# Chunk 0 of a scan stacked on 128 partitions, weight bits in PSUM, and last outputs on two queues, in a fused scan and two-MLP kernel

## The chip, the cores and the metric

One core of a Trainium2 chip. The metric is the device time of one launch in microseconds; the kernel before takes 570.02 us (median of three runs, 569.48 to 570.22).

## The reference

An attention-like scan over 4 batches, 8 heads, 768 positions, head size 32 and state size 16, then two MLPs over the 3072 tokens, width 256, hidden width 2048:

```python
L  = np.exp(cum[:, :, :, None] - cum[:, :, None, :]) * causal   # cum: running sum of log a
M  = np.einsum('bhin,bhjn->bhij', Cc, Bc) * L
y  = M @ xc + (Cc @ state) * np.exp(cum)                        # chunk by chunk
state = decay_full * state + sum_j(Bc_j x_j * decay_from_j)
h  = x @ w_in;  x = (h / (1 + np.exp(-1.702 * h))) @ w_out      # first MLP, x = y of all heads
h  = x @ w_in;  out = (h * np.clip(h + 3, 0, 6) / 6) @ w_out    # second MLP
```

Inputs of the scan are float32; the weights of the MLPs arrive as float64.

## The kernel before

**The scan.** The 768 positions are cut into 8 chunks of 96, so that there are 32 pieces q = 4c + b (chunk c, batch b), each with all 8 heads. A piece works on E = 112 rows: 96 positions of the chunk and the 16 rows of the state. Per piece and group g of four heads: `decay` (DVE, L450) makes the 112 x 448 matrix of decays by a scan over the row of `a`, with a constant pattern `pat_sb` that restarts it; for the first six pieces the row is spread over the partitions by four matmuls (`a_spread`, L440) into PSUM, for later ones by a DMA into SBUF. `s_mm` (PE, L485) makes the scores of two pieces. They are multiplied with the decays by DVE (`g_mul`, L488) or copied by ACT (`g_copy`, L491) and multiplied by POOL (`g_pool`, L495). `y_mm` (PE, L511) makes y and the new state; ACT copies the state (`y_state`, L525) and the high part of y (`y_out`, L545) and DVE makes the low part (`y_lo`, L557); `st_turn` (DVE, L561) transposes the state for the next chunk. In chunk 0 all of a piece's 112 rows are worked, over all 112 columns, though rows 96 to 111 hold no state yet (`zero_xs`) and the part below the diagonal of a causal matrix is zero.

**The MLPs.** The 3072 tokens are cut into blocks of 512. Everything is kept in two parts (high and low, both read by PE as fp32r), so that a product is three matmuls. The first blocks go in *units*, one of 16 weight slices with one block: `l1` (L672, 6 matmuls: low x with high weight, high x with high weight, high x with low weight), an activation chain (`act_chain`, ACT L675, L684 and DVE or POOL L687), and `l2` (L697, 6 matmuls); later blocks go in a Strassen-like form (L833). A weight slice p is loaded by SP (`w_load`, L353, 512 KB) and decoded: `w_scale` (ACT, L357), `w_low` (ACT L362 or DVE L364: the three bits that the float32 needs of the second word), `w_join` (DVE, L368: shifts and joins both words, two SBUF operands), `w_top` (L371, ACT, DVE or POOL), `w_bottom` (POOL, L375).

```python
low = raw(p)[:, :, 0]                                                        # L361
nc.vector.scalar_tensor_tensor(B_(f"dec:{p}"), t[:, :, 1], 3, t[:, :, 0], ALU.logical_shift_left, ALU.bitwise_or)   # L368
```

**The order.** `Schedule.run` is a list scheduler that runs when the program is built: each step is added with engine, estimated length, due time (`PIECE`, `tu`, `DL`, `TH`, `TL`) and what it reads and writes, and the steps of each engine stand in the order it finds. Buffers come from small pools; PSUM has two banks `h`, four `acc`, one `s` and one `y`. `decode(p, ...)` adds the steps of a slice.

**The start and the end.** Before the first piece, ACT issues the loads of the constants and of four row tables (L398, L400, L465) and loads its function table (L389); 12 warm-up matmuls run on PE. At the end, `outs` (L860 to L872) scales the two halves of each block's result (`o_scale`: ACT L853, DVE L855) and stores them (`o_store`, L858), on SP, the last half's first 256 columns on ACT.

## Time and profile before

| | |
|---|---|
| median of three runs | 570.02 us |
| the profiled execution | 570.0 us, span 568.2 us |
| mean granted TensorE clock | 0.985 |
| busy: PE, DVE, ACT, POOL | 553.7 (97%), 427.8 (75%), 331.3 (58%), 299.2 (53%) us |
| busy DMA, whole span | 37.7 MB, 66 GB/s on average |

The span is what the profiler saw of the program; 1.8 us of the launch lie outside it. A busy PE is one with matmuls in flight. A clock of 1.00 is 2.4 GHz, 0.50 is 1.2 GHz.

### The profile page before, as it was taken

How to read it: one execution, taken by the hardware profiler on the slowest of the kernel's cores; microseconds unless marked ns; L12 is line 12 of the kernel's file. 1: busy time of each engine (PE TensorE's matmuls, PEld its weight loads, DVE VectorE, ACT ScalarE, POOL GpSimd, SP SyncE). 2: the span in 40 equal slices, each digit the busy share in tenths (PEclk: the TensorE clock that was granted, in tenths of full speed). 3: DMA queues.
4: the chain of work that ended last, by engine and by line, in shares of the span. 5: the costliest groups of instructions: out<-in, count | busy, mean ns of one | idle time of the engine just before them, and what ended most of it. 6: DMA issues, size and time to landing. Idle time of an engine off the chain costs nothing.

```text
span 568.2 us, 8940 instructions
## 1 busy us (share of the span) xinstructions
PE 553.7 (97%) x3292; PEld 449.5 (79%) x3292; DVE 427.8 (75%) x617; ACT 331.3 (58%) x608; POOL 299.2 (53%) x281
## 2 busy tenths in 40 slices
...
GB/s 172 386 175 192 84 99 85 42 114 74 91 84 161 62 2 0 181 100 18 37 2 114 109 37 1 0 2 1 75 1 1 0 1 0 76 1 1 0 1 74
DMA packets 21995, 37.71 MB, mean 66 GB/s; under 512 B 10544, under 2 KB 14112, under 8 KB 21952
## 3 DMA queue, kind: packets, MB, share of 16 engines
...
q10 hardware_dynamic: 1136, 0.48, 0.4%
q8 instruction: 26, 0.43, 0.3%
q14 instruction: 17, 0.14, 0.1%
...
## 4 chain that ended last, share of the span: by engine, by line
PE 93%; DVE 3%; DMA 2%; ACT 1%; issue 1%; SPq 0%; DVEq 0%; ACTq 0%
PE acc L697 46%; PE h L833 19%; PE h L672 15%; PE s L833 4%; PE y L833 4%; PE s L485 2%; PE h L511 1%; DVE dec L368 1%; DMA bx_w<-in_wu 1%; DMA ov_a<-in_bcz 1%; DVE ov_a L450 1%; PE s L511 0%; PE y L511 0%; PE acc L485 0%; PE acc L672 0%
## 5 line engine op out<-in xcount | busy, mean ns | idle before, releaser
L687 POOL TENSOR_TENSOR gl<-gg,gh 128x512 fp32r<-128x512 f32 x42 | 60.8, 1447 | 96.2 <-ACT gh L684 40.5
L697 PE MATMUL acc<-gh,wl 128*128 128x512 f32 x256 | 100.1, 391 | 0.0
L697 PE MATMUL acc<-gh,wh 128*128 128x512 f32 x256 | 99.8, 390 | 0.0
L845 DVE TENSOR_TENSOR ov_b<-h,ov_b 128x512 f32<-128x512 f32 x64 | 44.1, 689 | 53.8 <-PE h L833 53.2
L697 PE MATMUL acc<-gl,wh 128*128 128x512 f32 x256 | 80.2, 390 | 0.5 <-DVE gl L687 0.5
L697 PE MATMUL acc<-ov_b,wh 128*128 128x512 f32 x256 | 78.8, 389 | 0.0
L450 DVE TENSOR_TENSOR_SCAN ov_a<-ov_a,pat_sb 112x448 f32<-112x448 f32 x52 | 65.6, 1298 | 0.0
L687 DVE TENSOR_TENSOR gl<-h,gh 128x512 fp32r<-128x512 f32 x60 | 41.0, 685 | 24.7 <-ACT gh L684 23.6
L687 POOL TENSOR_TENSOR ov_b<-ov_b 128x512 fp32r<-128x512 f32 x24 | 31.6, 1316 | 49.6 <-ACT ov_b L684 49.5
L697 PEld LDWEIGHTS acc<-gl,wh 128*128 128x128 f32 x256 | 48.0, 188 | 10.9 <-DVE gl L687 0.9
L697 PEld LDWEIGHTS acc<-gh,wl 128*128 128x128 f32 x256 | 48.0, 188 | 10.5 <-issue 0.2
L697 PEld LDWEIGHTS acc<-ov_b,wh 128*128 128x128 f32 x256 | 48.1, 188 | 10.0
L697 PEld LDWEIGHTS acc<-gh,wh 128*128 128x128 f32 x256 | 48.1, 188 | 9.9
L375 POOL TENSOR_TENSOR wl<-dec,wh 128x512 fp32r<-128x512 f32 x32 | 44.5, 1393 | 19.0 <-ACT wh L371 14.4
L678 ACT ACTIVATE gg<-h 128x512 f32<-128x512 f32 x48 | 28.7, 598 | 42.6 <-PE h L833 36.0
L675 ACT ACTIVATE h<-h 128x512 f32<-128x512 f32 x44 | 25.6, 583 | 45.2 <-PE h L672 35.8
L697 PE MATMUL acc<-ov_b,wl 128*128 128x512 f32 x128 | 49.8, 389 | 0.0
L684 ACT CAST gh<-gg 128x512 fp32r<-128x512 f32 x66 | 40.9, 620 | 11.8 <-DVE gg L681 10.6
L684 ACT CAST gh<-h 128x512 fp32r<-128x512 f32 x60 | 35.2, 588 | 16.2 <-DVE h L681 13.9
L687 POOL TENSOR_TENSOR ov_b<-gg,ov_b 128x512 fp32r<-128x512 f32 x16 | 21.1, 1319 | 43.1 <-ACT ov_b L684 30.7
L675 ACT ACTIVATE gg<-h 128x512 f32<-128x512 f32 x34 | 20.3, 598 | 38.9 <-PE h L672 38.5
L368 DVE SCALAR_TENSOR_TENSOR dec<-bx_w 128x512 uint32<-128x512 uint32 x32 | 34.3, 1079 | 3.2 <-ACT bx_w L357 1.8
(262 smaller groups left out, 1314.3 us busy)
## 6 DMA issues: line engine op xcount, KB each, us to landing
...
```

The lines of the kernel that those rows point to most:

```text
L368: nc.vector.scalar_tensor_tensor(B_(f"dec:{p}"), t[:, :, 1], 3, t[:, :, 0], ALU.logical_shift_left, ALU.bitwise_or)
L375: e.tensor_tensor(out=lo, in0=B_(f"dec:{p}").bitcast(F32), in1=hi.bitcast(F32), op=ALU.subtract)
L450: nc.vector.tensor_tensor_scan(t, a, pat_sb, 0.0, ALU.mult, ALU.add)
L485: nc.tensor.matmul(out=s_bank(q, g)[:, k, :], lhsT=t[r:r + NS, 0, i], rhs=t[r:r + NS, 1, i], start=True, stop=True)
L672: nc.tensor.matmul(out=B_(hn(u)), lhsT=w[:, 128 * j:128 * j + 128], rhs=x[:, j], start=x is xl and j == 0, stop=low and j == 1)
L675: nc.scalar.activation(B_(dst), B_(src), AF.Gelu_apprx_sigmoid)
L678: nc.scalar.activation(B_(dst), B_(src), AF.Relu, bias=3.0)
L684: nc.scalar.copy(B_(dst), B_(src))
L687: e.tensor_tensor(out=B_(dst), in0=B_(src), in1=B_(hi).bitcast(F32), op=ALU.subtract)
L697: nc.tensor.matmul(out=B_(acc[d]), lhsT=w[:, 256 + 128 * d:384 + 128 * d], rhs=g, start=first and d not in seen, stop=last and d not in [v ...
L833: nc.tensor.matmul(out=B_(dst), lhsT=w, rhs=x, start=start and i == 0, stop=i == 2, skip_group_check=True)
L845: nc.vector.tensor_tensor(out=B_(dst), in0=B_(a), in1=B_(b), op=ALU.add)
```

## The change

1. **Chunk 0 in stacked rows.** For its four pieces, rows 0 to 63 of two batches are stacked on 128 partitions (`x_spread` PE L488, `x_decay` DVE L517 with the pattern `patx`, `sx_mm` PE L535, `gx_mul` DVE L548 or `gx_copy` ACT L551 and `gx_pool` POOL L554). Rows 64 to 95 of all four batches are stacked on 128 partitions and only columns 64 to 111 are worked (`y_spread` L495, `y_decay` L520 with `paty`, `sy_mm` L544, `gy_mul` L557). `yx_mm` (PE, L569) makes y of two batches with 64 small matmuls into the banks h, h, s and y. New constants: `patx` by an ACT DMA (L422), `paty_sb` by another (L424) and `paty_spread` on POOL (L416), three selectors cast by ACT (`sel_rows`, L480), `ay_part` (ACT, L472). `pat_sb` moves behind these. ACT now loads a function table twice. The load of x is three DMAs (`x0_load`), `zero_xs` goes.
2. **Low bits in PSUM.** For slices 0 to 8 `w_low` writes the bits to bank s or y (`w_bits`), and `w_join` reads one operand from there. The scheduler's mark for steps that exclude POOL is off for these joins.
3. **Order.** `l1` of unit 0 is split: high x first, then low x, then the low weight. Pieces 6 to 9 are visited one by one (`SOLO`) and not in pairs. Several due times and choices of engine change (`PK`, `WAFTER`, `DL`, `TH`, `TL`, `GMS`, `TOPV`); `l2` of the last blocks is split by output half.
4. **Last outputs.** The second-last block's ACT half is stored by ACT's queue; the last block's halves change engines and are each cut in columns 128 to 511 (SP) and 0 to 127 (SP and ACT).

The core of the diff (the decays, scores and products of chunk 0, part 1, are shown by their adds and two functions):

```diff
 
 
-DL = (4.5, 1.3, 0.6, 1.6, 0.6)
-TOPV = (2, 5, 8, 11)
-TOPP = (2, 3, 7, 24, 27, 28, 31)
+LP = 9
...
-UGAP = (12, 0.25)
+P0 = (4.8, 9.0)
...
     i = (q >= 12) + (q >= 16) + (q >= 22)
     return PK[2 * i] + PK[2 * i + 1] * (q - (6, 12, 16, 22)[i])
 
-WAFTER = (2.9, 4.9, 6.9, 11.0, 13.0, 15.0, 17.0)
+WAFTER = (2.4, 4.5, 5.1, 9.7, 10.0, 17.7, 22.7)
 TURN = 30.0
 HACC = (2, 3)
...
+    def w_bits(p):
+        return B_(f"{'sy'[p % 2]}:low{p}").bitcast(U32) if p < LP else raw(p)[:, :, 0]
+
     def w_low(p, act):
-        low = raw(p)[:, :, 0]
+        low = w_bits(p)
         if act:
             nc.scalar.activation(low, raw(p).bitcast(U8)[:, :, 3], AF.Copy, scale=1 / 32, bias=-31 / 64)
         else:
-            nc.vector.tensor_scalar(low, low, 29, None, ALU.logical_shift_right)
+            nc.vector.tensor_scalar(low, raw(p)[:, :, 0], 29, None, ALU.logical_shift_right)
 
     def w_join(p):
         t = raw(p)
-        nc.vector.scalar_tensor_tensor(B_(f"dec:{p}"), t[:, :, 1], 3, t[:, :, 0], ALU.logical_shift_left, ALU.bitwise_or)
+        nc.vector.scalar_tensor_tensor(B_(f"dec:{p}"), t[:, :, 1], 3, w_bits(p), ALU.logical_shift_left, ALU.bitwise_or)
 
     def w_top(p, e):
...
+            nc.scalar.dma_start(out=patx(), in_=pat[0:64, 0:4 * E].bitcast(BF16).unsqueeze(0).to_broadcast([2, 64, 4 * E]))
+        elif i == 3:
+            nc.scalar.dma_start(out=paty_sb, in_=pat[0:32, 0:E - 64].bitcast(BF16).unsqueeze(0).to_broadcast([4, 32, E - 64]))
         else:
             nc.scalar.dma_start(out=idn_sb, in_=idn)
 
     add("POOL", 0.3, -90, zero_state, w=["st_sb"])
     add("POOL", 0.35, -75, selectors, r=["idn"], w=["sel"])
     add("-", 0.0, -95, lambda: None, w=["att"])
...
+    def sel_rows(i):
+
+        nb, q0 = ((2, 0), (2, 2), (NB, 0))[i]
+        src = idn_sb[0:NB * 4, NS + NH + 4 * q0:NS + NH + 4 * q0 + 4 * nb].rearrange("r (b q) -> r q b", q=4).unsqueeze(3).to_broadcast([NB * 4, 4, nb, 128 // nb])
+        nc.scalar.copy(B_(SX[i])[0:NB * 4].rearrange("r (q b n) -> r q b n", q=4, b=nb), src)
+
+    def sel_of(i, qh):
+        return B_(SX[i])[0:NB * 4, 128 * qh:128 * qh + 128]
+
+    def x_spread(p, g):
+        for i in range(2):
+            for part in range(2):
+                nc.tensor.matmul(out=B_(f"acc:lx{p}.{g}")[:, 2 * E * i:2 * E * i + 256], lhsT=sel_of(p, 2 * g + i),
+                                 rhs=B_("gh:acl")[0:NB * 4, 256 * part:256 * part + 256], start=part == 0, stop=part == 1)
...
+    def yx_mm(p):
+
+        x = B_("xs:0")
+        for g in range(2):
+            for late in range(2):
+                for k in range(4):
+                    h = 4 * g + k
+                    for b in (2 * p, 2 * p + 1):
+                        r, n, c, i = (32 * b, 32, 64, 2) if late else (64 * (b % 2), 64, 0, p)
+                        gm = gmy()[r:r + n, h, :] if late else gmx(p, g)[r:r + n, k, :]
+                        nc.tensor.matmul(out=y_view(b)[32 * k:32 * k + 32, g, c:E], lhsT=x[r:r + n, i, h * D:(h + 1) * D], rhs=gm,
+                                         start=not late, stop=bool(late), skip_group_check=True)
 
     def a_spread(q, g):
...
+        if q < NB and b % 2 == 0:
+            p = q // 2
+            t = KX[p]
+            sch.take(f"l:x{p}", t)
+            for g in range(2):
+                add("PE", 0.48, t - 1 + 0.1 * g, x_spread, p, g, r=["gh:acl", "al", SX[p]], new=[f"acc:lx{p}.{g}"])
+                add("DVE", 1.06, t + 0.1 * g, x_decay, p, g, r=[f"acc:lx{p}.{g}", f"l:x{p}", "gg:patx"], w=[f"lx{p}.{g}"])
+            add("PE", 1.0, t + 0.9, sx_mm, p, r=["r16:0"] + rows[0], new=[SBANK(q, g) for g in range(2)])
+            for g in range(2):
+                sn, gn = SBANK(q, g), f"gm:x{p}.{g}"
+                if 2 * p + g in GMX:
+                    add("ACT", 0.55, t + 1.2 + 0.1 * g, gx_copy, p, g, r=[sn], new=[gn])
+                    add("POOL", 1.16, t + 1.2 + 0.1 * g, gx_pool, p, g, r=[f"l:x{p}", f"lx{p}.{g}"], w=[gn])
+                else:
...
         R, Dn, W = f"bx:w{p}", f"dec:{p}", f"wt:{p}"
         k -= DL[4] if p < NM else 0.0
+        low = dict(new=[f"{'sy'[p % 2]}:low{p}"]) if p < LP else dict(w=[f"low{p}"])
         add("SP", 0.4, k - 9, w_load, p, new=[R], kb=512, after=after)
         add("ACT", 0.72, k - DL[0], w_scale, p, r=[R], w=[f"hi{p}"])
         if LOW(p) == "ACT":
-            add("ACT", 0.70, k - DL[1], w_low, p, True, r=[R], w=[f"low{p}"])
-        else:
-            add("DVE", 0.45, k - DL[1] - 0.4, w_low, p, False, r=[R], w=[f"low{p}"], port=True)
-        add("DVE", 0.75, k - DL[2], w_join, p, r=[R, f"hi{p}", f"low{p}"], new=[Dn], port=True)
+            add("ACT", 0.70, k - DL[1], w_low, p, True, r=[R], **low)
+        else:
...
-        add("PE", 4 * MM, t, l1, u, False, r=[W, f"bx:{k}h", f"bx:{k}l", *parts[k]], new=[h])
-        add("PE", 2 * MM, t - 50, l1, u, True, r=[W, f"wl{m}", f"bx:{k}h"], w=[h])
+        if u:
+            add("PE", 4 * MM, t, l1, u, None, r=[W, f"bx:{k}h", f"bx:{k}l", *parts[k]], new=[h])
+        else:
+            add("PE", 2 * MM, t, l1, u, 1, r=[W, f"bx:{k}h", *[x for x in parts[k] if x[-1] == "h"]], new=[h])
...
     def outs(k, t):
+
+        end = k >= NB6 - 2
         for d in range(2):
-            end = k == NB6 - 1 and d == 1
-            for f, g, e in ((0, BW // 2, "ACT"), (BW // 2, BW, "DVE")) if end else ((0, BW, ("ACT", "DVE")[d]),):
+            e = "ACT" if d == (k == NB6 - 1) else "DVE"
+            cuts = [(128, BW, "SP"), (0, 128, ("SP", "ACT")[d])] if k == NB6 - 1 else [(0, BW, "ACT" if end and e == "ACT" else "SP")]
+            for f, g, q in cuts:
                 o = o_name(k, d, f)
                 sch.take(o, t)
-                add(e, 0.1 + 0.00104 * (g - f), t, o_scale, k, d, f, g, e, r=[f"acc:B{k}.{d}", o], w=[f"{o}.{f}"])
+                add(e, 0.08 + (0.00102 if e == "ACT" else 0.00119) * (g - f), t, o_scale, k, d, f, g, e, r=[f"acc:B{k}.{d}", o], w=[f"{o}.{f}"])
                 a = LO[k] + f
                 while a < LO[k] + g:
                     b = min(LO[k] + g, T * (a // T + 1))
-                    q = "ACT" if end and f == 0 else "SP"
-                    add(q, 0.4, t + 0.5, o_store, k, d, a // T, a, b, f, q, r=[o, f"{o}.{f}"], w=[f"out{k}.{d}.{a}"], kb=(b - a) // 2)
+                    add(q, 0.43, t + 0.5, o_store, k, d, a // T, a, b, f, q, r=[o, f"{o}.{f}"], w=[f"out{k}.{d}.{a}"], kb=(b - a) // 2)
                     a = b
 
```

**Orders.** DVE, from the joins of the first weight slices to the low parts of the first token block, before (`acc`, `s`, `y` are PSUM banks, `bx_w` raw weight words, `dec` joined weights, `bx_0h` and `bx_0l` the parts of the first token block):

```order
L368 SCALAR_TENSOR_TENSOR dec_103<-bx_w_183 128x512
L368 SCALAR_TENSOR_TENSOR dec_104<-bx_w_189 128x512
L364 TENSOR_SCALAR bx_w_218<-bx_w_218 128x512
L450 SCALAR_TENSOR_TENSOR ov_a<-acc_129,pat_sb 112x448
L557 TENSOR_TENSOR bx_0l<-acc_132,bx_0h 128x2x192
L450 SCALAR_TENSOR_TENSOR ov_a<-acc_130,pat_sb 112x448
L488 TENSOR_TENSOR ov_a<-s_133,ov_a 112x448
L488 TENSOR_TENSOR ov_a<-y_134,ov_a 112x448
L368 SCALAR_TENSOR_TENSOR dec_105<-bx_w_218 128x512
L368 SCALAR_TENSOR_TENSOR dec_106<-bx_w_256 128x512
L557 TENSOR_TENSOR bx_0l<-acc_131,bx_0h 128x2x96
L557 TENSOR_TENSOR bx_0l<-acc_131,bx_0h 128x2x32
```

and with the change:

```order
L625 TENSOR_TENSOR ov_a<-acc_130,ov_a 112x448
L694 TENSOR_TENSOR bx_0l<-s_134,bx_0h 128x2x96
L694 TENSOR_TENSOR bx_0l<-y_135,bx_0h 128x2x96
L625 TENSOR_TENSOR ov_a<-acc_131,ov_a 112x448
L698 STREAM_TRANSPOSE ov_a<-st_sb 32x4x32 x4
L625 TENSOR_TENSOR ov_a<-acc_133,ov_a 112x448
L380 TENSOR_SCALAR s_134<-bx_w_195 128x512
L384 SCALAR_TENSOR_TENSOR dec_103<-bx_w_195,s_134 128x512
L384 SCALAR_TENSOR_TENSOR dec_104<-bx_w_202,y_135 128x512
L380 TENSOR_SCALAR s_134<-bx_w_231 128x512
L694 TENSOR_TENSOR bx_0l<-acc_130,bx_0h 128x2x96
L694 TENSOR_TENSOR bx_0l<-acc_130,bx_0h 128x2x32
```

Ahead of the last L557 (now L694) stood four joins; now two stand there, each with a PSUM bank as an operand, and no scan does. From the first scan to there, twelve scans of 448 columns have become eight and one of 384.

ACT, from its first instruction, before:

```order
L398 DMA pat_sb<-in_pat 112x448
L400 DMA idn_sb<-in_idn 128x40
L465 DMA ov_a<-in_bcz 16x8x112 x4
L389 ACT_TABLE_LOAD
L389 ACTIVATE st_tr<-st_sb 128x1
L491 COPY ov_a<-h_127 112x448
L491 COPY ov_a<-h_128 112x448
L357 ACTIVATE bx_w_183<-bx_w_183 128x512
```

and with the change:

```order
L422 DMA gg_108<-in_pat 128x1x448
L602 DMA ov_a<-in_bcz 16x8x112 x4
L424 DMA paty_sb<-in_pat 128x1x48
L480 ACT_TABLE_LOAD
L480 CAST gh_111<-idn_sb 16x512
L480 CAST gl_114<-idn_sb 16x512
L472 CAST gl_113<-gh_110 16x2x2x47
L480 CAST gh_112<-idn_sb 16x512
L420 DMA pat_sb<-in_pat 112x448
L402 ACT_TABLE_LOAD
L402 ACTIVATE st_tr<-st_sb 128x1
L551 COPY ov_a<-h_128 128x448
```

Ahead of the first copy of scores now stand two more DMA issues, a second table load and four casts; the load of `pat_sb` is moved from first place behind the casts.

POOL, around the low parts of the first weights (`wl`; `wh` are the high parts), before:

```order
L495 TENSOR_TENSOR ov_a<-ov_a 112x448 x6
L375 TENSOR_TENSOR wl_72<-dec_103,wh_71 128x512
L495 TENSOR_TENSOR ov_a<-ov_a 112x448 x2
L375 TENSOR_TENSOR wl_74<-dec_104,wh_73 128x512
L473 COPY ov_a<-idn_sb 128x16x16
L371 CAST wh_75<-dec_105 128x512
L371 CAST wh_77<-dec_106 128x512
L375 TENSOR_TENSOR wl_76<-dec_105,wh_75 128x512
L375 TENSOR_TENSOR wl_78<-dec_106,wh_77 128x512
```

and with the change:

```order
L691 TENSOR_TENSOR bx_0l<-gg_109,bx_0h 128x2x96
L691 TENSOR_TENSOR bx_0l<-gg_107,bx_0h 128x2x96
L632 TENSOR_TENSOR ov_a<-ov_a 112x448
L610 COPY ov_a<-idn_sb 128x16x16
L391 TENSOR_TENSOR wl_72<-dec_103,wh_71 128x512
L391 TENSOR_TENSOR wl_74<-dec_104,wh_73 128x512
L387 CAST wh_75<-dec_105 128x512
L387 CAST wh_77<-dec_106 128x512
L391 TENSOR_TENSOR wl_76<-dec_105,wh_75 128x512
L391 TENSOR_TENSOR wl_78<-dec_106,wh_77 128x512
```

The low parts of slices 0 and 1 stood between products of pieces; now they stand behind all of them and behind the copy of L610, one after the other.

At the end, the last two blocks' stores were seven on SP and two on ACT; now SP has five (two of 256 columns, then 384, 128, 384), and ACT three: two of 256 columns right behind its scaling of the second-last block, and one of 128 at the very end.

## Rows read from the trace of the kernel before

**Rows 1.** Page of the profile: the chain that ended last, by engine.

```profile
PE 93%; DVE 3%; DMA 2%; ACT 1%; issue 1%; SPq 0%; DVEq 0%; ACTq 0%
```

**Rows 2.** Windows: us, busy PE PEld DVE ACT POOL, PE clock, DMA share, GB/s.

```profile
24.00:32.00 8.00, 5.20 (x41) 3.00 (x41) 7.67 (x12) 6.14 (x14) 7.97 (x8) 0.50 1.03 362
...
240.00:400.00 160.00, 160.00 (x704) 132.00 (x705) 121.58 (x170) 114.82 (x208) 121.00 (x119) 1.00 0.12 40
```

**Rows 3.** Timeline of DVE, start: start us, us, line, operation, [idle before <-releaser].

```profile
5.38 4.03 DVE L450 TENSOR_TENSOR_SCAN ov_a<-acc,pat_sb 112x448 f32<-112x448 f32 x4 [1.08 <-PE acc L440]
...
10.38 4.02 DVE L450 TENSOR_TENSOR_SCAN ov_a<-acc,pat_sb 112x448 f32<-112x448 f32 x4
...
15.72 0.56 DVE L557 TENSOR_TENSOR bx_0l<-acc,bx_0h 128x384 fp32r<-128x384 f32 x1 [1.31 <-ACT bx_0h L545]
...
19.95 4.03 DVE L368 SCALAR_TENSOR_TENSOR dec<-bx_w 128x512 uint32<-128x512 uint32 x2
...
27.20 0.61 DVE L488 TENSOR_TENSOR ov_a<-y,ov_a 112x448 f32<-112x448 f32 x1
27.73 1.28 DVE L368 SCALAR_TENSOR_TENSOR dec<-bx_w 128x512 uint32<-128x512 uint32 x2
29.34 0.49 DVE L557 TENSOR_TENSOR bx_0l<-acc,bx_0h 128x192 fp32r<-128x192 f32 x2 [0.33 <-ACT bx_1h L545]
29.94 3.46 DVE L368 SCALAR_TENSOR_TENSOR dec<-bx_w 128x512 uint32<-128x512 uint32 x1
```

**Rows 4.** Groups of DVE instructions, first 37 us: operation, count, busy us, mean ns, idle before.

```profile
L364 DVE TENSOR_SCALAR bx_w<-bx_w 128x512 uint32<-128x512 uint32 x2 | 0.8, 412 | 0.0
```

**Rows 5.** Timeline of ACT, start; ACTq are DMA issues.

```profile
1.67 2.90 ACTq L465 DMA_DIRECT2D ov_a<-in_bcz  x4
4.61 1.28 ACT L389 ACT_TABLE_LOAD   x1 [4.61 <-issue]
...
29.17 0.71 ACT L357 ACTIVATE bx_w<-bx_w 128x512 f32<-128x512 f32 x1
29.74 0.71 ACT L362 ACTIVATE bx_w<-bx_w 128x512 uint32<-128x512 uint8 x1
```

**Rows 6.** DMA issues of ACT's queue, 1.6 to 2.0 us: KB, us to landing.

```profile
ov_a<-in_bcz ACTq DMA_DIRECT2D x1, 56.0 KB, 3.6
```

**Rows 7.** Timeline of PE, start.

```profile
13.02 1.19 PE L440 MATMUL acc<-gh,sel 128*112 128x256 f32 x8
...
22.79 2.05 PE L440 MATMUL acc<-gh,sel 128*112 128x256 f32 x8
...
29.98 1.19 PE L672 MATMUL h<-bx_0l,wh 128*128 128x512 f32 x2 [1.51 <-DVE bx_0l L557]
30.96 1.05 PE L672 MATMUL h<-bx_0h,wh 128*128 128x512 f32 x2
```

**Rows 8.** Timeline of POOL: start us, us, line, operation, [idle before <-releaser].

```profile
9.59 2.24 POOL L495 TENSOR_TENSOR ov_a<-ov_a 112x448 f32<-112x448 f32 x2 [5.22 <-ACT ov_a L491]
...
29.21 1.17 POOL L371 CAST wh<-dec 128x512 fp32r<-128x512 f32 x2
30.35 2.51 POOL L375 TENSOR_TENSOR wl<-dec,wh 128x512 fp32r<-128x512 f32 x2
```

**Rows 9.** Timeline of PE, pieces visited within the units.

```profile
63.46 0.97 PE L511 MATMUL s<-ov_a 112*32 112x112 f32 x32
64.36 0.73 PE L672 MATMUL h<-bx_0l,wh 128*128 128x512 f32 x2
...
80.36 0.59 PE L511 MATMUL y<-ov_a 112*32 112x112 f32 x16
```

**Rows 10.** Timeline of all engines, end.

```profile
560.98 0.60 ACT L853 ACTIVATE ov_b<-acc 128x512 f32<-128x512 f32 x1 [1.56 <-PE acc L697]
...
562.38 3.27 SPq L858 DMA_DIRECT2D out<-ov_b  x7
```

**Rows 11.** Window of half a microsecond at the end, columns as in rows 2.

```profile
565.00:565.50 0.50, 0.00 (x0) 0.00 (x0) 0.00 (x0) 0.00 (x0) 0.00 (x0) 0.83 1.03 307
```

More of the change, by code (lines that the diff above doesn't have):

```diff
@@ new lines, in y_spread, with lx, ly @@
+    def y_spread():
+        w = 2 * (E - 64)
+        for qh in range(4):
+            for part in range(2):
+                nc.tensor.matmul(out=B_("acc:ly")[:, w * qh:w * qh + w], lhsT=sel_of(2, qh),
+                                 rhs=B_("gl:acl")[0:NB * 4, 128 * part:128 * part + w], start=part == 0, stop=part == 1)
+    def lx(p, g):
+        return lf_b[sch.slot[f"l:x{p}"]][:, 4 * E * g:4 * E * g + 4 * E].rearrange("p (k e) -> p k e", k=4)
+    def ly():
+        return lf_b[sch.slot["l:y"]][:, 0:NH * (E - 64)].rearrange("p (h e) -> p h e", h=NH)
@@ new lines, in sy_mm, with gx_mul @@
+    def sy_mm():
+        t = rows16(0)
+        for k in range(4):
+            for b in range(NB):
+                for g in range(2):
+                    r, i = 64 * (b % 2) + 32 * g, 4 * (b // 2) + k
+                    nc.tensor.matmul(out=sy(g)[32 * b:32 * b + 32, k, :], lhsT=t[r:r + NS, 0, i, 64:CH], rhs=t[r:r + NS, 1, i, 64:E],
+                                     start=True, stop=True)
+    def gx_mul(p, g):
+        nc.vector.tensor_tensor(out=gmx(p, g), in0=sx(p, g), in1=lx(p, g), op=ALU.mult)
```

161 lines of the change are left out of this document (126 added, 35 removed).

## The prediction

> **What bounds the kernel now.** I read the chain of waits first: TensorE holds 93% of it [rows 1], and a window from 240 to 400 us is filled by matmuls to the last tenth, 704 of them at the full clock, 0.227 us each [rows 2]. No other engine's work there can shorten the span; a unit of 12 matmuls takes 12 x 0.227 = 2.73 us whatever the rest does. So this change can only move three things: when the first unit starts, what the pieces' visits cost between the units, and what comes after the last matmul.
>
> *Start.* The timeline of PE shows that the first matmul of unit 0 starts at 29.98 us and was released by the low part of y on DVE, after 1.51 us of waiting [rows 7]. DVE starts on chunk 0 at 5.38 us [rows 3] and the low part ends at 29.98 + about 0.05 = 30.03 us, taking the release as immediate: 24.65 us, of which the rows show only 1.31 and 0.33 us idle [rows 3]; 23.0 us is work. Before unit 0, **DVE is the bound**. The two joins at 19.95 us took 4.03 us and the one at 29.94 us 3.46 us, where the pair at 27.73 us took 1.28 us, 0.64 each [rows 3]. What differs is POOL, which multiplies or subtracts beside the slow ones; a scan with one PSUM and one SBUF operand is not slowed beside such work: four take 4.03 us alone at 5.38 us and 4.02 us at 10.38 us [rows 3], where POOL's products of 9.59 to 11.83 us lie beside them [rows 8].
>
> *Clock.* The granted clock is 0.50 (1.2 GHz) from 24 to 32 us [rows 2]: eight spreading matmuls take 2.05 us at 22.79 us and took 1.19 us at 13.02 us, and the first two matmuls of unit 0 last 30.96 - 29.98 = 0.98 us for 0.45 [rows 7].
>
> *End.* SP issues seven stores from 562.38 to 565.65 us, 0.47 each, though ACT had scaled a half at 560.98 + 0.60 = 561.58 us [rows 10]. The transfers run at 307 GB/s with the DMA engines all busy [rows 11].
>
> **The change, part by part.** The sum is made against the profiled execution, 570.0 us (span 568.2 and 1.8 outside); the median is 570.02 us, so the same difference holds.
>
> *First scan, later by 3.1 us.* ACT's four row loads end at 1.67 + 2.90 = 4.57 us [rows 5]. The issue for the Y pattern waits for the first of them, which lands 3.6 us after its issue, at 5.3 us [rows 6]: issue over at 5.7 us. Then a table load, 1.28 us [rows 5], to 7.0 us, a selector cast of about 0.55 us, and the spread, for which DVE waited 1.08 us before [rows 3]; four matmuls for the first bank, so 1.0 us: 8.5 us against 5.38 us. Bounds: 7.9 us (the wait costs nothing) and 9.1 us (another cast must go first).
>
> *DVE's work, less by 6.2 us.* Four scans fewer and one of 384: -4 x 1.01 + 0.86 = -3.2 us. Products: four of 448 stay, two of 192 are new, 0.3 each as half of a 448 product of 0.61 [rows 3]: +0.6. The low parts of pieces 0 and 1 go to POOL, those of 2 and 3 are two halves of the 0.56 us: -0.5. Two joins instead of four stand ahead of the last low part: 5.31 (4.03 + 1.28) becomes 2 x 0.69 = 1.4: -3.9. Two low-bit steps that write PSUM stand in for two of 0.41 us [rows 4]; the trace shows no such write, so between 0.41 and the 0.69 of a full-width join with two operands; I take 0.6, nearest the wider: +0.4. The join with a PSUM operand is not shown either: at best 0.54, at worst 2.0 (as 4.03 / 2, if it still waits for POOL); I take 0.69, since the scan beside POOL is the nearest row. Sum -6.6; I keep 0.4 back for dependent starts: -6.2, so 23.0 - 6.2 = 16.8 us.
>
> *DVE idle, 2.5 us.* The same hand-offs as before, 1.64 us, and one spread of eight matmuls at the lower clock, 2.05 - 1.19 = 0.86 us [rows 7], since PE now stands idle from the warm-up to the selectors. Bounds: 0 and 1.64 + 3 x 0.86 = 4.2 us.
>
> The last low part is then ready at 8.5 + 16.8 + 2.5 = 27.8 us, **2.2 us earlier**. Unit 0's two high matmuls, 0.98 us, now go before it. They need slice 0's high part, cast by ACT behind the join: 27.8 - 0.77 (last low parts) - 0.6 - 0.69 = 25.7, so 26.4 us; they fit but for a little. I take 0.9 us: **-3.1 us** for the start.
>
> *POOL's low weights, +0.5 us.* POOL had four in hand early; now slices 0 and 1 follow each other from 26.4 to 29.0 us (1.26 each), two casts (1.17) to 30.15 and the next two low parts (2.51) to 32.7 us [rows 8]. Unit 2's last two matmuls want the third, ready at 31.4 us, at 26.9 + 2.75 + 1.42 + 0.9 = 32.0 us. The slack is half a microsecond; a hold-up costs between 0 and one operation, 1.26 us. I take 0.5.
>
> *Visits of pieces 6 to 9, +0.65 us.* A pair holds PE for 0.97 us, one piece for 0.59 us; the matmul behind a visit is longer by 0.11 us (0.73 for 0.62) [rows 9]. Per pair 2 x 0.59 - 0.97 + 0.11 = 0.32, twice.
>
> *End, -0.8 us.* Five SP issues from 562.38 us end at 562.38 + 5 x 0.47 = 564.7 us for 565.65: -0.95 if the issues bound. The bytes are the same (two blocks, 1.05 MB, 3.4 us at 307 GB/s) and their first store goes out at 561.58 instead of 562.38 us: -0.8 if the transfers bound, and the DMA share of 1.03 [rows 11] says they do. The Trainium skill's page "DMA: Bandwidth & Descriptors", section "Issuing engines are not separate DMA queues", speaks against more: transfers started by any engine run on the same 16 DMA engines, so issuing from several saves the sequencer's time alone. By that rule the second queue shortens no transfer and the sum stays at -0.8; by issue times alone it would be 0.15 us lower.
>
> *At nothing:* the three x loads and the later pattern of 112 rows land beside the scans of chunk 0; without that cover they cost DVE an idle time already in the bounds. The second table load lies beside the first scans; uncovered it costs 1.28 us. The split of the last products changes no matmul.
>
> Sum: -3.1 + 0.5 + 0.65 - 0.8 = -2.75: 567.25 us of 570.0, and with the median **567.3 us**.
>
> **Rivals.**
>
> *DVE never starves.* Idle 0 instead of 2.5, low weights in time, end by issue times: -5.6 + 0.65 - 0.95 = -5.9: 564.1 us. For it: DVE was busy for 23.0 of 24.65 us. Against it: PE has more small matmuls per scan now, at the lower clock.
>
> *The start's gain is eaten.* First scan at 9.1 us and idle of 4.2: start gain 3.1 - 0.6 - 1.7 = 0.8; -0.8 + 0.5 + 0.65 - 0.8 = -0.45: 569.6 us. For it: ACT's chain ahead of the first spread is long and each of its links can slip; all four casts wait behind the one table load.
>
> *The joins are not freed.* If a join with a PSUM operand waits for POOL as before, each takes 2.0 us: 2 x 1.3 = 2.6 us later: -2.75 + 2.6: 569.9 us. The scan's rows speak against it.
>
> *ACT falls behind, and the change loses.* Before, ACT did 14 steps of decoding ahead of the first activation; now six stand there, and eight must be made up. Its steps follow at 0.57 us (29.17 to 29.74) [rows 5], 8 x 0.57 = 4.5 us. In each unit ACT has two activation steps and up to three of decoding, 5 x 0.57 = 2.85 us against 2.73 us of PE: it can't catch up while slices are decoded, and PE waits for weights. -3.1 + 4.5 + 0.65 - 0.8 = +1.25: **571.3 us**. It decides as soon as units wait for more than 2.75 us in all. Against it: weights that come later by what units need later cost nothing, and the order puts each step by a due time.
>
> **How the numbers follow.** The forecast has 0.50 (its own range 566.0 to 569.0 us), starvation-free 0.14, eaten 0.18, joins 0.07, ACT behind 0.11. A measurement tells about 0.2%, 1.1 us, from no change: 568.9 to 571.2 us is the same. Faster: 0.46 of the forecast, all of the first rival, 0.04 of the eaten: 0.64. Same: 0.04 + 0.14 + 0.07 - 0.02 for joins that cost more + 0.01 of ACT's case: 0.24. Slower: 0.10 + 0.02 = 0.12. The range 564.3 to 570.3 us leaves out half of the first rival, 0.07, and ACT's case with a little of the joins', 0.12.
>
> **What would show it.** The first DVE scan at 8.5 us; joins at 0.69 us beside POOL's work, and none above 1; the first L1 matmul near 27 us, with the high part of x; no PE gaps over 0.5 us from then to 80 us; 16 matmuls per visit four times between 45 and 62 us; the last issue near 564.7 us. The forecast is wrong if the first L1 matmul comes after 29.5 us, or if PE waits for `wl` or `wh` in the first units by more than 2 us.

## The result and the profile after

The changed kernel takes **576.51 us** (median of four runs, 575.82 to 577.5) against 570.12 us (569.48 to 570.31): 1.0115 times as long, 95% interval 1.0096 to 1.0135. The forecast was 567.3 us with 564.3 to 570.3 as its range: wrong in sign. The profiled execution took 575.95 us with a span of 574.2 us, 6.0 us above that of before. The medians of this document leave out two executions that took far longer, one of experiment 7 (1944.77 us) and one of the kernel before (927.27 us).

TensorE still holds the chain that ended last; the row that answers to [rows 1], on the page of the profile after:

```profile
PE 94%; DMA 2%; DVE 1%; ACT 1%; ACTq 1%; issue 0%; SPq 0%; DVEq 0%
```

So the 6.0 us came from ahead of the units, between them, or behind them. The timeline of ACT at the start (answering to [rows 5]) shows the first loss:

```profile
1.19 1.14 ACTq L422 DMA_DIRECT2D gg<-in_pat  x1
2.37 6.20 ACTq L602 DMA_DIRECT2D ov_a<-in_bcz  x4
8.62 0.62 ACTq L424 DMA_DIRECT2D paty_sb<-in_pat  x1
9.26 1.28 ACT L480 ACT_TABLE_LOAD   x1 [9.26 <-DMA ov_a<-in_bcz]
10.56 0.62 ACT L480 CAST gh<-idn_sb 16x512 fp32r<-16x512 f32 x1
```

The four row loads held ACT's queue for 6.20 us, where they took 2.90 us before; they stand behind the load of the pattern `patx`, whose source is read twice (`unsqueeze(0).to_broadcast([2, 64, ...])`). Behind a table load the selectors' casts start, at 10.56 us. Windows of the same stretch (us, busy PE, PEld, DVE, ACT, POOL, PE clock, DMA share, GB/s) show how little moved meanwhile:

```profile
4.00:6.00 2.00, 0.00 (x0) 0.00 (x0) 0.08 (x1) 0.00 (x0) 0.00 (x0) 1.00 0.71 146
...
7.00:8.00 1.00, 0.00 (x0) 0.00 (x0) 0.00 (x0) 0.00 (x0) 0.00 (x0) 1.00 0.15 43
```

A share of 0.15 of 16 DMA engines is 2.4 engines; by queue, 1.4 of them (8.8%) worked for ACT's loads and the rest for a load of x on SP's queue. The timeline of DVE (columns as in [rows 3]):

```profile
12.50 4.03 DVE L517 TENSOR_TENSOR_SCAN ov_a<-acc,gg 128x448 f32<-128x448 f32 x4 [8.42 <-PE acc L488]
...
22.95 0.62 DVE L557 TENSOR_TENSOR gg<-acc,ov_a 128x192 f32<-128x192 f32 x2 [2.40 <-PE acc L544]
...
28.84 0.62 DVE L625 TENSOR_TENSOR ov_a<-acc,ov_a 112x448 f32<-112x448 f32 x1 [2.32 <-PE acc L622]
...
33.15 0.69 DVE L384 SCALAR_TENSOR_TENSOR dec<-bx_w,s 128x512 uint32<-128x512 uint32 x1
...
35.66 0.23 DVE L694 TENSOR_TENSOR bx_0l<-acc,bx_0h 128x64 fp32r<-128x64 f32 x1 [0.33 <-ACT bx_1h L682]
```

The first scan runs at 12.50 us, not 5.38. The join at 33.15 us takes 0.69 us. Every longer wait of DVE is now for PE: 8.42 us, in which PE itself waits for the selectors, then 2.40 and 2.32 us. The timeline of PE (answering to [rows 7]) shows why:

```profile
11.27 3.75 PE L488 MATMUL acc<-gh,gh 16*128 16x256 f32 x16 [7.43 <-ACT gh L480]
...
22.85 2.05 PE L577 MATMUL acc<-gh,sel 128*112 128x256 f32 x8
...
30.90 2.71 PE L648 MATMUL acc<-ov_a 112*32 112x112 f32 x32 [1.98 <-DVE ov_a L698]
34.99 1.22 PE L849 MATMUL h<-bx_0h,wh 128*128 128x512 f32 x2 [1.37 <-ACT bx_0h L682]
36.01 1.15 PE L849 MATMUL h<-bx_0l,wh 128*128 128x512 f32 x2
...
41.19 0.39 PE L875 MATMUL acc<-gh,wl 128*128 128x512 f32 x1
```

Unit 0 starts at 34.99 us, 5.01 us later than before. Between the selectors and 29 us PE has no gap; here is that window after the change:

```profile
11.30:29.00 17.70, 17.62 (x328) 14.85 (x328) 10.44 (x13) 6.91 (x20) 5.02 (x6) 1.00 0.89 220
```

and the stretch from the first scan to unit 0 in the kernel before:

```profile
5.40:30.00 24.60, 17.21 (x237) 12.19 (x236) 22.80 (x32) 13.15 (x31) 15.45 (x13) 0.78 1.03 316
```

Before, DVE was busy for 22.80 of 24.60 us and PE for 17.21. Now PE is busy for 17.62 of 17.70 us and DVE for 10.44: **the bound has changed engines**. PE runs 328 matmuls there, up to some 26 us at the lower of its two rates: eight spreads take 2.05 us, as at 22.79 us before, and not 1.19 [rows 7]. The 32 score matmuls at 27.77 us are faster again, 1.15 us for 1.85 of the same 32 in experiment 1. The clock column reads 1.00 in this window; the durations of the spreads say otherwise, and I go by them.

The end did what it should (timeline of the last microseconds, answering to [rows 10]):

```profile
568.55 0.86 ACTq L1040 DMA_DIRECT2D out<-ov_b  x2
...
569.33 2.31 SPq L1040 DMA_DIRECT2D out<-ov_b  x5
```

Five SP issues take 2.31 us where seven took 3.27 [rows 10], and the span ends 4.28 us after the last matmul (which ends at 569.92 us) instead of 5.22 (562.98).

### The profile page after: what moved, and what is told of

Read it like the earlier page. It is cut to its first block, busy times and chain, and to the rows that moved or that the text cites. A ratio compares the mean times of both kernels' runs of the same rounds, so it can differ in the third digit from the quotient of the medians.

```text
span 574.2 us, 9178 instructions
## 1 busy us (share of the span) xinstructions
PE 557.5 (97%) x3412; PEld 453.2 (79%) x3412; DVE 428.4 (75%) x621; ACT 333.8 (58%) x622; POOL 288.9 (50%) x278
## 4 chain that ended last, share of the span: by engine, by line
PE 94%; DMA 2%; DVE 1%; ACT 1%; ACTq 1%; issue 0%; SPq 0%; DVEq 0%
PE acc L875 45%; PE h L1015 19%; PE h L849 15%; PE s L1015 4%; PE y L1015 4%; PE s L622 2%; PE h L648 1%; DMA bx_w<-in_wu 1%; DMA ov_a<-in_bcz 1%; PE acc L577 1%; PE acc L488 1%; PE acc L849 0%; PE s L648 0%; PE acc L622 0%; PE h L569 0%; PE h L535 0%
## 5 line engine op out<-in xcount | busy, mean ns | idle before, releaser
L865 POOL TENSOR_TENSOR gl<-gg,gh 128x512 fp32r<-128x512 f32 x53 | 73.5, 1388 | 146.7 <-PE h L1015 72.2
L587 DVE TENSOR_TENSOR_SCAN ov_a<-ov_a,pat_sb 112x448 f32<-112x448 f32 x52 | 68.3, 1345 | 0.3 <-DMA ov_a<-acl_d 0.3
L862 ACT CAST gh<-gg 128x512 fp32r<-128x512 f32 x77 | 47.8, 621 | 19.9 <-DVE gg L859 18.5
L865 DVE TENSOR_TENSOR gl<-h,gh 128x512 fp32r<-128x512 f32 x49 | 33.4, 684 | 30.2 <-ACT gh L862 30.0
L391 POOL TENSOR_TENSOR wl<-dec,wh 128x512 fp32r<-128x512 f32 x32 | 43.3, 1356 | 23.7 <-ACT wh L387 19.6
L856 ACT ACTIVATE gg<-h 128x512 f32<-128x512 f32 x48 | 28.7, 598 | 44.3 <-PE h L1015 35.4
L853 ACT ACTIVATE h<-h 128x512 f32<-128x512 f32 x41 | 23.9, 583 | 42.2 <-PE h L849 32.7
L853 ACT ACTIVATE gg<-h 128x512 f32<-128x512 f32 x37 | 22.1, 598 | 41.9 <-PE h L849 41.3
L862 ACT CAST gh<-h 128x512 fp32r<-128x512 f32 x49 | 28.7, 585 | 7.8 <-DVE h L859 5.5
L1027 DVE TENSOR_TENSOR h<-h,ov_b 128x512 f32<-128x512 f32 x32 | 22.4, 699 | 8.3 <-PE h L1015 8.1
L859 DVE SCALAR_TENSOR_TENSOR gg<-gg,h 128x512 f32<-128x512 f32 x40 | 27.1, 678 | 1.7 <-ACT gg L856 1.3
```

The source lines that it names most:

```text
L391: e.tensor_tensor(out=lo, in0=B_(f"dec:{p}").bitcast(F32), in1=hi.bitcast(F32), op=ALU.subtract)
L587: nc.vector.tensor_tensor_scan(t, a, pat_sb, 0.0, ALU.mult, ALU.add)
L853: nc.scalar.activation(B_(dst), B_(src), AF.Gelu_apprx_sigmoid)
L856: nc.scalar.activation(B_(dst), B_(src), AF.Relu, bias=3.0)
L859: nc.vector.scalar_tensor_tensor(out=B_(dst), in0=B_(g), scalar=6.0, in1=B_(h), op0=ALU.min, op1=ALU.mult)
L862: nc.scalar.copy(B_(dst), B_(src))
```

## The experiments

Each kernel's time is a median beside runs of the kernel before on the same chip (570.0 to 570.2 us); the interval is the 95% interval of the ratio to it. Edits of "the change" start from the changed kernel, edits of "before" from the other.

**1. The pattern as two plain loads** (of the change).

```diff
-            nc.scalar.dma_start(out=patx(), in_=pat[0:64, ...].unsqueeze(0).to_broadcast([2, 64, 4 * E]))
+            for j in range(2):
+                nc.scalar.dma_start(out=patx()[64 * j:64 * j + 64], in_=pat[0:64, ...])
```

> The changed kernel, but the 128-row pattern is loaded by two plain loads of 64 rows instead of one broadcast load. Theory A (the broadcast load runs on one or two DMA engines at 40 to 48 GB/s, lands late, and ACT's last row load, the second pattern, the table load and the selector casts queue behind it): ACT's four row loads are issued by about 5.5 us instead of 8.57, the first DVE scan starts at 8.5 to 9.7 us instead of 12.5, the units some 3 us earlier, time 572.5 to 573.5 us. Theory B (the row loads themselves are slow, or the casts): first scan not before 11.5 us, time within 1 us of 576.

573.62 us, ratio 1.0064 (1.0051 to 1.0078): 2.9 us off the change's time. Timelines of ACT, DVE and PE of this version:

```profile
2.44 2.86 ACTq L603 DMA_DIRECT2D ov_a<-in_bcz  x4
```
```profile
9.72 4.03 DVE L518 TENSOR_TENSOR_SCAN ov_a<-acc,gg 128x448 f32<-128x448 f32 x4 [5.75 <-PE acc L489]
...
27.50 0.62 DVE L626 TENSOR_TENSOR ov_a<-acc,ov_a 112x448 f32<-112x448 f32 x1 [3.75 <-PE acc L623]
```
```profile
8.49 3.75 PE L489 MATMUL acc<-gh,gh 16*128 16x256 f32 x16 [4.65 <-ACT gh L481]
...
33.64 1.22 PE L850 MATMUL h<-bx_0h,wh 128*128 128x512 f32 x2 [1.37 <-ACT bx_0h L683]
```

The row loads take 2.86 us again and the first scan comes 2.78 us earlier: the read-twice load was the cause of ACT's hold-up. But unit 0 comes only 1.35 us earlier: DVE now waits 3.75 us for PE further on. A second cause stands behind the first. The last matmul comes 2.41 us earlier than in the change (566.90 for 569.31): of unit 0's pairs of matmuls only three and a part run at the lower rate here, in the change five and a part, so that the first 16 take 5.23 us for 6.20.

**2, 3. Longer warm-up**: `WARM = 12` becomes 70 (in the change) and, with experiment 1's edit, 50. The count also enters the scheduler's estimate, so both plans came out in another order.

> The changed kernel with 70 warm-up matmuls instead of 12, so that PE works until close to 11 us; nothing else. Theory C (PE, idle from 3.85 to 11.27 us, runs chunk 0 and the first units at the lower clock, and DVE's 6.4 us of idle time up to the last low part of y come from that): the first scan stays at 12.3 to 13 us, the eight-matmul spread falls from 2.05 to about 1.2 us, DVE's idle time to 3 us or less, unit 0's pairs to 0.45 us apart, time 570.5 to 572.5 us. If theory A is all of it (a late start merely shifts everything), time within 1 us of 576.

> Both edits: two plain pattern loads, and 50 warm-up matmuls. If A and C hold together, the first scan is at about 9 us, the first unit's first matmul at 26 to 28 us at the full clock, time 566 to 569 us, below the kernel before. If only one of them holds, 571 us or more.

582.26 us, ratio 1.0216 (1.02 to 1.0232), and 574.27 us, 1.0071 (1.0057 to 1.0085). The first sixteen spreads took 2.45 us instead of 3.75 in both, the second ones 2.05 us again, at a granted clock of 0.50. In the first, unit 0 started only at 40.75 us, waiting for a high weight. As the order changed with the count, they decide nothing about the clock; experiment 11 repeats the test without that.

**4. The new end alone** (before, with `outs` of the change).

> The kernel before with the changed function of the last outputs alone (second-last block's ACT half stored by ACT's queue, last block cut at 128 columns, halves on the other engines). Forecast's term: 0.8 us less than before, about 569.2 us, with the bound by issue times at 0.95. Rival (the transfers already filled the engines, so a second queue gives nothing): within 0.2 us of before.

569.15 us, ratio 0.9982 (0.9973 to 0.999): faster by about 1.0 us. The term of the end was real, and alone it is a gain.

**5. The bits in PSUM alone** (before, with part 2).

> The kernel before with part 2 alone: the low bits of slices 0 to 8 in PSUM banks, joins read them there. Theory D (the joins of 4.03 and 3.46 us come from their two SBUF operands beside POOL): every join 0.68 to 0.70 us, the last low part of y some 2 us earlier (4.03 + 1.28 becomes 2.8, two low-bit steps dearer by 0.28), time 567.5 to 568.5 us. Rival (the bits' step waits for a score or y bank and gives the gain back): within 0.5 us of before.

571.79 us, ratio 1.0027 (1.0016 to 1.0039): slower, outside both expectations. The joins take what was forecast, this one beside POOL's work of 28.15 to 30.67 us (timeline of DVE):

```profile
29.68 0.68 DVE L372 SCALAR_TENSOR_TENSOR dec<-bx_w,y 128x512 uint32<-128x512 uint32 x1
```

and unit 0 starts at 29.12 us, 0.86 us earlier. The loss comes later, among the pieces. Waits of PE from 42 to 110 us (the kernel before shows none there):

```profile
PE h L677 <- DVE bx_1l L561: 1.1, 1, 1.1
PE y L515 <- POOL ov_a L499: 0.4, 1, 0.4
```

DVE's scans whose two operands are both in SBUF are what grew (groups of DVE, 44 to 92 us: count, busy us, mean ns, idle). Before:

```profile
L450 DVE TENSOR_TENSOR_SCAN ov_a<-ov_a,pat_sb 112x448 f32<-112x448 f32 x12 | 15.5, 1308 | 0.0
```

with the change:

```profile
L587 DVE TENSOR_TENSOR_SCAN ov_a<-ov_a,pat_sb 112x448 f32<-112x448 f32 x12 | 16.6, 1395 | 0.0
```

with the bits alone:

```profile
L454 DVE TENSOR_TENSOR_SCAN ov_a<-ov_a,pat_sb 112x448 f32<-112x448 f32 x15 | 24.1, 1624 | 0.0
```

A scan rose from 1308 to 1624 ns there (three scans more fall into the window in that order). My reading is that a join which no longer waits for POOL lets the next two-operand step meet POOL instead; as the order changed with the edit, no run shows that by itself. The SBUF page of the Trainium skill ("SBUF — State Buffer", section "Who interferes with whom") has the rule: a DVE step with two inputs in SBUF contends with POOL's reads, and one with at most one such input, outside the two-port modes, doesn't. Joins at 0.68 us and scans at 1624 ns beside each other agree with it.

**6. Pairs again for pieces 6 to 9** (of the change).

```diff
-SOLO = (0, 1, 3, 4, 5)
+SOLO = (0, 1, 5)
```

> The changed kernel with pieces 6 to 9 visited in pairs again. The forecast's term for their single visits is 0.65 us: time 575.5 to 576.2 us, against 576.5. Rival (the lag that grows by 1.0 us between 41 and 100 us comes from weights or the activation chain, not from visits): no change within 0.3 us, and matmuls of the units still wait for DVE's low parts.

580.89 us, ratio 1.0187 (1.0164 to 1.021). Both expectations missed: the pairs cost 4.4 us. But the order was planned anew and unit 0 came at 36.05 us, so 1.06 us arose ahead of any visit, and PE waited 1.4 us for a product and 1.0 us for a low part. The run doesn't price the visits; it shows that this plan is not better with pairs.

**7. The selectors cast by POOL and DVE** (experiment 1, and the casts of `sel_rows` and `ay_part` off ACT, planned anew).

```diff
...
-        nc.scalar.copy(B_(SX[i])[0:NB * 4].rearrange(...), src)
+        (nc.gpsimd, nc.vector, nc.gpsimd)[i].tensor_copy(B_(SX[i])[0:NB * 4].rearrange(...), src)
...
```

> The changed kernel with two plain pattern loads, and the three selector casts and the copy beside them on POOL and DVE, which stand idle then, instead of ACT behind its DMA issues and table load. Theory A (ACT's chain ahead of the first spread is the cause, not the stacked rows): first scan at 5.5 to 6.5 us, PE never idle for over 2 us ahead of it, units 5 to 7 us earlier than in the changed kernel, time 567 to 570.5 us, no slower than the kernel before. Theory E (chunk 0's stacked form costs PE and its hand-offs more than it saves on DVE, however early it starts): the span from the first scan to unit 0 stays at 22 us or more, time 571 us or more.

573.75 us (three runs, 573.71 to 576.59, the last of which lifts the ratio), ratio 1.0087 (1.0057 to 1.0116). The first scan runs at 5.64 us, and PE works nearly without a gap from 3.98 us to the end of the scores at 22.01. Unit 0 starts at 28.49 us, 1.49 us earlier than before and 6.50 earlier than in the change, so the late selectors were worth most of that. From the first scan to unit 0 it is still 22.85 us, as the second theory said, and the kernel is slower: its last matmul starts 4.78 us later than before (567.15 for 562.37). PE, busy for 56.00 of 56 us from 44 to 100 us before, is busy for 53.40 here. The windows in which it stands, columns as above:

```profile
68.00:76.00 8.00, 7.23 (x71) 5.08 (x70) 8.00 (x12) 3.17 (x8) 6.35 (x4) 1.00 0.26 57
76.00:84.00 8.00, 6.17 (x77) 4.20 (x79) 7.43 (x13) 3.03 (x7) 5.36 (x9) 1.00 0.25 98
```

DVE is full there, 15.43 of 16 us for 13.89 before, though over the whole stretch it worked less than in the change (49.88 us for 50.75). PE's longest wait is 1.41 us for a product of DVE at 83.69 us; behind it the granted clock reads 0.59 from 84 to 88 us. **In this order a gain at the start doesn't reach the end.**

**8. The bits and the end** (before, with parts 2 and 4).

> The kernel before with parts 2 and 4 alone (low bits in PSUM, last outputs on two queues), without the stacked chunk 0 and without the new due times. If the gains add: 1.0 us for the end and some 2 us for the joins, 566.5 to 567.5 us, faster than both kernels. If the joins give nothing: 569.1 us.

571.07 us, ratio 1.0015 (1.0006 to 1.0024): neither expectation, but the end's gain, not quite whole (0.7 us for 1.0), on top of the loss of experiment 5. Within the interval the two add up.

**9. The first scan as early as before**: patterns and `paty` ahead of the row loads, the casts on POOL and DVE, the order of the change kept but for these.

```diff
+            for j in range(2):
+                nc.scalar.dma_start(out=patx()[64 * j:64 * j + 64], in_=pat[0:64, ...])
+            nc.scalar.dma_start(out=paty_sb, in_=pat[0:32, ...])
...
-        nc.scalar.copy(ay()[:, :, :, 1:E - 64], ...)
+        nc.vector.tensor_copy(ay()[:, :, :, 1:E - 64], ...)
...
```

> The changed kernel with the planned order left as it is; only the front: both patterns and their loads issued first (two plain loads of 64 rows and the small one), the selector casts and the copy beside them made by POOL and DVE at the same places of the program. Theory A alone (the late front is the whole loss): first scan at 5.5 to 6.5 us, unit 0 at 28 to 29 us, 6 to 7 us earlier, and the time follows: 569.5 to 570.5 us. Theory F (an earlier start is taken back where DVE is full, about 60 to 92 us, as the runs with part 2 alone and with the re-planned selectors suggest): unit 0 as early, DVE busy 7.8 of 8 us in stretches between 60 and 92 us and PE waiting there for 1 us or more, time 571 to 573.5 us.

574.07 us, ratio 1.0074 (1.0059 to 1.0089). Timelines of DVE and PE:

```profile
5.40 4.03 DVE L519 TENSOR_TENSOR_SCAN ov_a<-acc,gg 128x448 f32<-128x448 f32 x4 [0.19 <-PE acc L490]
...
15.17 0.62 DVE L550 TENSOR_TENSOR ov_a<-h,ov_a 128x448 f32<-128x448 f32 x1 [4.61 <-PE h L537]
...
27.11 0.62 DVE L627 TENSOR_TENSOR ov_a<-acc,ov_a 112x448 f32<-112x448 f32 x1 [3.74 <-PE acc L624]
```
```profile
13.40 1.72 PE L537 MATMUL h<-ov_a 16*64 16x112 f32 x26 [3.34 <-DMA ov_a<-in_bcz]
...
33.24 1.22 PE L851 MATMUL h<-bx_0h,wh 128*128 128x512 f32 x2 [1.37 <-ACT bx_0h L684]
```

The first scan is 7.1 us earlier than in the change, and unit 0 only 1.75 us (33.24 for 34.99). A row load, now behind the patterns, held PE until 13.40 us; from 15 to 27 us PE is busy for 12.00 of 12.00 us and DVE for 5.30. Both theories expected unit 0 at 28 to 29 us and missed; the waits of theory F didn't come either, PE is busy for 32.00 of 32 us from 60 to 92 us.

**10. The end, and unit 0's high x first** (experiment 4, with the two matmuls of high x ahead of those of low x in unit 0; order unchanged).

```diff
+        high = high[2:] + high[:2] if u == 0 else high
```

> The kernel before with the new last outputs and, in unit 0 alone, the two matmuls with the high x ahead of those with the low x, in an unchanged planned order. The high part is there at 29.3 us and the low part at 30.03: unit 0 ends 0.5 to 0.7 us earlier. If a gain at the start passes to the end: 568.4 to 568.7 us. Theory F (it is lost behind it): 569.1 us, as with the last outputs alone.

568.92 us, ratio 0.9984 (0.9975 to 0.9993). The fastest of all, but against experiment 4 (0.9982, 0.9973 to 0.999) no difference that can be told. Unit 0 starts at 28.78 us, 1.20 us earlier, and the last matmul starts 0.36 us earlier (562.01 for 562.37).

**11. More warm-up, same order** (experiment 1, four times the warm-up matmuls in the same step).

```diff
         for _ in range(n):
+            for _ in range(4):
```

> The run with two plain pattern loads, and four times as many warm-up matmuls (48) with the planned order unchanged. Theory C (PE at the lower rate makes DVE wait in chunk 0): first scan at 9.3 to 9.7 us as there, the eight-matmul spreads at 1.2 us instead of 2.05, DVE's idle time up to the last low part down by 2 us or more, time 570.5 to 572.5 us. Rival (the granted clock is taken away during chunk 0 when PE worked before it, as in both earlier warm runs at 12 to 15 us): spreads again 2.05 us, time 572.5 to 575 us.

574.8 us, ratio 1.0084 (1.007 to 1.0097). Timeline of PE:

```profile
8.57 2.28 PE L490 MATMUL acc<-gh,gh 16*128 16x256 f32 x16
...
12.69 2.05 PE L579 MATMUL acc<-gh,sel 128*112 128x256 f32 x8
...
25.68 2.05 PE L624 MATMUL acc<-ov_a 16*112 16x112 f32 x29 [1.21 <-issue]
...
33.57 1.22 PE L851 MATMUL h<-bx_0h,wh 128*128 128x512 f32 x2 [1.37 <-ACT bx_0h L684]
```

and of DVE, the scan that PE waits for before its second eight spreads:

```profile
17.07 1.09 DVE L589 TENSOR_TENSOR_SCAN ov_a<-acc,pat_sb 112x448 f32<-112x448 f32 x1 [2.33 <-DMA pat_sb<-in_pat]
```

The first spreads run at the full rate (2.28 us for 3.75); by 12.69 us eight take 2.05 us again, and the granted clock reads 0.50 from 16 to 32 us. What PE gained ahead (2.76 us at 12.69) it lost in two waits: 0.82 us for this scan, which waited for the load of `pat_sb` that the change moved back, and 1.21 us at 25.68 us, which the profile ties to nothing. This warm-up doesn't give chunk 0 the full rate.

**12. Half of the spreads' matmuls** (experiment 1; the second matmul of each spread, which adds the low part of the row of a, left out, so the decays lose their low bits).

```diff
-            for part in range(2):
+            for part in range(1):
...
```

> Edit: the version with the pattern in two plain loads, and each spread of the rows of a (x, y and the four of chunk 1's first pieces) without its second matmul, which adds the low part of the row: 24 matmuls on TensorE instead of 48 in the spreads before unit 0, the order of every engine unchanged. The decays lose their low bits; nothing else is left out. In the version it starts from, TensorE stands without a gap from 8.49 to about 27.5 us, at 2.05 us for eight spreads, and DVE waits 1.32 and 3.75 us for it. The removed matmuls took 3.75/2 + 1.77/2 + 2 x 2.05/2 = 4.8 us there. Theory TE (in the stacked chunk 0 TensorE, and not DVE, sets the start of unit 0): the products of scores for pieces 4 and 5 come some 4 us earlier, DVE's wait of 3.75 us before the products nearly goes, the first L1 matmul comes at 29.5 to 31 us for 33.64, and the time is 569.5 to 571.5 us for 573.6. Rival L (loads, the late pattern of 112 rows above all, or DVE's own work set it): the first L1 matmul stays at 32.5 us or later, TensorE shows new waits for DVE or for loads that sum to the 4 us, and the time is 572.5 us or more. Between them (31 to 32.5 us): both are within 2 us of each other.

571.68 us, ratio 1.0029 (1.0019 to 1.0038). Timeline of PE:

```profile
8.48 2.46 PE L489 MATMUL acc<-gh,gh 16*128 16x256 f32 x8 [4.63 <-ACT gh L481]
...
22.53 1.90 PE L623 MATMUL acc<-ov_a 16*112 16x112 f32 x32
...
30.54 1.22 PE L850 MATMUL h<-bx_0h,wh 128*128 128x512 f32 x2 [1.37 <-ACT bx_0h L683]
```

The scores at 22.53 us stood at 25.63 us in experiment 1, and unit 0 comes at 30.54 for 33.64 us: both 3.10 us earlier. DVE's list is the same in both. Of the 4.8 us of matmuls taken out, 3.1 came through; PE now waits 0.7 us for a scan, which waited 2.01 us for `pat_sb`. What PE saved up to the scores came out at unit 0. Theory TE holds for the start, though DVE's wait before the products stayed at 3.15 us, which it had nearly gone. The time fell by 1.9 us of the 3.1 (the medians are up to 1 us from single runs, the profiled span fell by 2.4) and lies 0.2 us above the range that it gave. In unit 0 five pairs run at the lower rate here instead of three, which is what the span lacks.

## Why the prediction was wrong

Step by step, against the profiled execution of before:

| step | forecast | measured |
|---|---|---|
| first scan | +3.1 | 12.50 - 5.38 = +7.1 |
| DVE's work up to the last low part | 16.8 us | 17.0 us |
| DVE idle there | 2.5 (0 to 4.2) | 6.4 |
| first matmul of low x | -2.2 | 36.01 - 29.98 = +6.0 |
| high x first | -0.9 | 36.01 - 34.99: -1.0 |
| start of unit 0 | -3.1 | +5.0 |
| low weights, visits, all up to the last matmul | +1.15 | +1.9 |
| end | -0.8 | -0.9 |

**"First scan, later by 3.1 us" failed in one link.** The forecast let ACT's row loads end at 4.57 us, as before; they ended at 2.37 + 6.20 = 8.57. From there to the first scan it allowed 8.5 - 4.57 = 3.93 us, and 12.50 - 8.57 = 3.93 us it was. That the two agree is luck: the issue of the Y pattern took 0.69 us for 1.13, the cast 0.71 for 0.55 and the spread 1.23 for 1.0, and the differences cancel. Missed was that the load ahead of them, `patx`, is a transfer of another kind. Experiment 1 shows it: two plain loads of the same bytes, and the queue took 2.86 us. The page "DMA: Bandwidth & Descriptors" of the Trainium skill, section "Rules for kernel authors", says that a leading broadcast of c copies confines a transfer to at most c DMA engines; the 1.4 engines that ACT's queue used from 7 to 8 us, for c = 2, agree. I costed that issue as one more issue.

**"Before unit 0, DVE is the bound" failed next, and it weighs as much.** That was true of the kernel before and was carried over to the changed one. DVE's work was forecast to 0.2 us (17.0 for 16.8), its idle time was not: 6.4 us, beyond the upper bound of 4.2, which allowed three spreads at the lower rate. From the first scan to unit 0 it took 34.99 - 12.50 = 22.49 us where the forecast had 26.9 - 8.5 = 18.4; the first scan was late by 4.0 us more than forecast, this stretch by 4.1. The rest of PE's work in chunk 0 was never summed. It is 328 matmuls in 17.62 us, and DVE's shorter list only meets PE's longer one sooner. Behind PE's last scores, at 27.77 us, stands a chain of hand-offs that wasn't summed either: products, turned state, y, high part, 7.2 us to unit 0 and 8.0 in experiments 1, 9 and 12. Experiments 1, 9 and 11 move the first scan to 9.72, 5.40 and 9.35 us and unit 0 starts at 33.64, 33.24 and 33.57 us; experiment 12 takes matmuls away and moves it by 3.10. In experiment 1 PE has no gap from 8.49 us to the scores, in experiment 9 none from 13.40 us on, once its row load is there, and in experiment 7, where PE starts at 3.98 us and isn't held, unit 0 comes at 28.49: PE sets the scores and with them unit 0. In experiment 11 it waits in between, 0.8 us for a scan held by the late `pat_sb` and 1.2 us for something unnamed. The late `pat_sb` is thus the next limit behind PE; whether there is another is open. How much of PE's list is the lower rate and how much the number of small matmuls is not separated either: experiment 11 could not hold the rate.

**The steps that held.** High x first, -1.0 for -0.9; joins at 0.69 us beside POOL, none slower among those with an operand in PSUM; the end, -0.9 for -0.8, nearer to the bound by issue times (-0.95), and experiment 4 measures it alone at 1.0 us. Why it reached that bound, where the full DMA share argued for the lower figure, wasn't tried.

**"Visits" and "low weights" came out too low, +1.9 for +1.15.** From the first matmul of unit 0 to the first of its second layer PE took 41.19 - 34.99 = 6.20 us against 35.52 - 29.98 = 5.54 before:

```profile
35.52 0.39 PE L697 MATMUL acc<-gh,wl 128*128 128x512 f32 x1
```

It did 16 matmuls in that time and 18 before. At 0.227 us each [rows 2] these are 3.63 and 4.09 us, so the lower rate cost 2.6 us for 1.45: 1.1 us, since five pairs and more run at it instead of three, a term that the forecast didn't have. That leaves 0.8 us for visits, waits and the rest. No matmul waited for a low weight, so that term of 0.5 came to nothing; PE's only named wait from 42 to 110 us is 0.4 us for the low part of an activation. What the visits cost by themselves isn't shown.

**No rival named it.** "The change loses" was there, by ACT falling behind its decoding. ACT did hold things up, but at 2.37 us, by a transfer and not by decoding steps, and no unit waited for weights. Its decoding steps ahead of the first activation, too, are 15 and 9 in the traces, not 14 and six. "The start's gain is eaten" names the right two places, first scan and idle time, but both passed its bounds (9.1 and 4.2 us). That DVE, freed of joins, would be held by PE stands only as a reason against the first rival and was priced nowhere.

**And a gain at unit 0 doesn't always reach the end.** The sum passed each microsecond at unit 0 on to the end, as no wait shows between the units before. Where the order stayed as it was, most came through: 2.4 of 3.1 us in the span of experiment 12; of the 1.20 us in experiment 10, 0.36 at the last matmul. Experiments 5 and 7 start unit 0 by 0.86 and 1.49 us earlier and end 1.6 and 3.6 us later. DVE's work in 44 to 100 us grew from 47.23 to 51.54 and 49.88 us of 56, and from 68 to 84 us it was full (15.90 and 15.43 of 16). Both have their own order, so what of it is POOL's contention with scans and what the order's is open.

A version faster than both kernels is the kernel before with the new end, 569.15 us, or with high x first as well, 568.92 us.
